# Weight-block sums formed on VectorE, their stores issued from GpSimd, token sums spread between products

## The chip, the cores and the metric

The kernel runs on one NeuronCore of a Trainium2 chip. Five engines work in parallel, each through its own instruction stream in order: TensorE (PE, the products), VectorE (DVE), ScalarE (ACT), GpSimd (POOL) and SyncE (SP, which here only issues DMAs). They meet through semaphores. The metric is the device time of one execution in microseconds (us), the median of the runs.

## The reference

Banded attention with distance biases on 4 batches, 8 heads, 768 positions and 64 elements a head, and then a feed-forward part on the 3072 tokens of 512 elements:

```python
scores = scale * np.matmul(q, k.transpose(0, 1, 3, 2)) + bias      # bias: -slope * distance
scores = np.where(keep, scores, -1000000000.0)                     # keep: first 8 keys, last 96 keys
a = np.exp(scores - max); a = a / (sum(a) + 1e-09)
x = (a @ v)                    # as 3072 x 512
h = (x @ w1) * (x @ w2) @ w3   # 512 -> 1024 -> 1024
out = h @ w_out                # 1024 -> 512
```

## The kernel before, in words

**Arithmetic.** Products are made of 32-bit values that are split in a high and a low half; a product of two such values is three products on TensorE (high by high, high by low, low by high). `w3 @ w_out` is multiplied out first (steps F), so a token needs only `x @ w1`, `x @ w2`, their elementwise product, and a product with the folded matrix.

**Units.** The tokens go in six units of 512. Units 0 and 1 multiply plainly: step `U.f.m.half` is half of the six 512-column products of feature block f (0 to 7) with `w1` (m = 0) or `w2` (m = 1). Results lie in a pool of four PSUM buffers (`m`); ScalarE copies the first (`gate`, tile `ag`), VectorE multiplies the second into it (`product`, L289), ScalarE and VectorE make its halves (`gh`, `gl`, L299). `Z.t.*` are the second products of the unit's t-th 128 tokens (L311 to L313), `ot` their copy and store. Units 2 to 5 (class `Sevenths`) use seven products of sums in place of eight: for that they need four sums of weight blocks (s1 to s4) beside the blocks, and sums of token blocks.

**Attention** runs ahead between the products. For score step s (two to a pair d = s // 2): `S.s` are the score products into the PSUM tiles `sc` and `more`, `R.s.q` the maxima on VectorE (L704), `E.s.q` the exponentials on ScalarE (L711), `s.s`, `c.s`, `X.s` the normalising and transposing on VectorE (L716, L717, L729, L737), and `V.d` the products with the values (L751), which leave x in `sc`. For units 0 and 1 `h.d` (ScalarE, L766) and `l.d` (VectorE, L771) make the halves `xh` and `xl`; only then may `sc` be overwritten by the next `S`. For later units `tokens(d)` copies x to `more_raws` and makes the blocks' sums and halves.

**Weight blocks.** In unit 0 each `w1`/`w2` block f is loaded, put together from 64-bit words (`convert`, L177 to L181), and split in halves `w12h`, `w12l`. Each is written to a DRAM buffer `ws` (`blocks_out`, four stores of 256 KB a block, on SP's queue). For the four sums, `rejoin(f)` adds the two halves back by two DMAs that GpSimd issues: one copies the high half to `block_sums`, the second adds the low half to it (L201, L202; the second waits for the first). `combine(f)` makes the four sums on VectorE (L208), ScalarE and VectorE halve them into `block_parts` (L211, L214), and `sums_out(f)` stores six pieces to `ws` on SP's queue (L219). `block_sums` has two buffers (f even, odd), `block_parts` holds the halves of one f. From unit 2 on `bring` loads blocks from `ws` (L239).

**Order.** TensorE's order is the program's order. Up to the end of unit 0 the table `ORDER` is the order on every engine, but a scheduler puts steps of later units between its steps where it takes an engine to be free. After it (`planned`) TensorE and ScalarE keep the written order; VectorE, SP and GpSimd are ordered by the scheduler. An engine that waits holds up all that stands behind the waiting instruction.

Of the kernel before, what the change touches and what calls it, by code (L numbers as in the profile page):

```python
# [20 lines left out]
P = 128  # L21
# [9 lines left out]
R = 32  # L31
# [53 lines left out]
class FeedForward:  # L85
# [485 lines left out]
def banded(ctx, tc, ff, ns, nt, n1, nf, oki, qk, vx, sc, pr):  # L571
# [203 lines left out]
    def tokens(d):  # L775

        u = d // 2
        raw = ff.tokens[:, d % 2]
        nc.scalar.activation(raw.rearrange("p (n t) -> p n t", t=T), sc[:, :, :T], AF.Copy)
        if d % 2 == 0:  # L780
            if u % 2 == 0:
                homes[u] = [ff.wf[1][:, k * 2048:(k + 1) * 2048] for k in range(4)]
            else:
                homes[u] = [xp.tile([P, 2048], F32R, tag=tag, name=f"{tag}{k}_{u}") for k in range(2) for tag in ("xh", "xl")]
        bh, bl, th, tl = homes[u]
        both = ff.tokens.rearrange("p d n -> p (d n)")
# [10 lines left out]
        halves(bh[:, 1024:1536], bl[:, 1024:1536], b22)  # L797
        halves(th[:, :512], tl[:, :512], b11)
        v.tensor_tensor(out=b12, in0=b22, in1=b12, op=ALU.subtract)
        v.tensor_tensor(out=b22, in0=b22, in1=b11, op=ALU.subtract)  # L800
        halves(th[:, 1024:], tl[:, 1024:], both[:, 1024:])
        v.tensor_tensor(out=b21, in0=b21, in1=b22, op=ALU.subtract)
        halves(th[:, 512:1024], tl[:, 512:1024], b21)
# [37 lines left out]

    def planned():

        def of(u, name):
            return lambda *x: getattr(units[u], name)(*x)

        last = NC // 2 - 1
        for f in range(NFC):
            for m in range(2):
                for half in range(2):  # L850
                    todo = [(of(1, "first"), f, m, half)]
                    if half:
                        todo += [(of(1, "gate"), f)] if m == 0 else [(of(1, x), f) for x in ("product", "high", "low")]
                    if m == 0 and half == 0:
                        todo.append((ff.blocks_out, f))
                    at = f * 4 + m * 2 + half
                    k = at // 5 + 1
                    if at % 5 == 0 and k < NFC:
                        todo.append((ff.combine, k))
                    if at % 5 == 1 and k < NFC:  # L860
                        todo += [(ff.sums_high, k), (ff.sums_low, k), (ff.sums_out, k)]
                        if k + 2 < NFC:
                            todo.append((ff.rejoin, k + 2))
                    if (f, m, half) in ((4, 0, 0), (7, 1, 1)):
                        todo += [(ff.bring, int(f == 7), g) for g in range(3)]
                    yield [("U", 1, f, m, half)] + todo
        for u in range(1, last + 1):
# [12 lines left out]
            for t in range(2 * T // P):  # L880
                for f in range(NFC):
                    todo = [(of(u, "third"), t, f)]
                    if f == NFC - 1:
# [4 lines left out]
                    if t == 0 and f in (1, 2) and tail:
                        yield tail.pop(0)
                    if t == 3 and f < 5 and u < last:  # L890
                        p = (1, 5, 6, 2, 7)[f]
                        yield [("P", u + 1, 0, p), (of(u + 1, "step"), p, 0)]

    with tc.manual_schedule(engines={mybir.EngineType.PE}):
        with tc.manual_schedule(engines={mybir.EngineType.DVE, mybir.EngineType.SP, mybir.EngineType.Activation, mybir.EngineType.Pool}):
            ordered()
        with tc.manual_schedule(engines={mybir.EngineType.Activation}):
# [22 lines left out]
            for d in range(STEPS // 2, n // 2):  # L920
                u = d // 2 - 1
                load(d)
                ahead = [s for s in (2 * d + 2, 2 * d + 3) if s < n]
                for s in ahead:
                    keys(s)
                rounds(d)
                go(place["Z", u, 2, 4] if d % 2 else place["U", u, 4, 0, 0] if u == 1 else place["P", u, 4, 1])
                values(d)
                tokens(d)
                if ahead:  # L930
                    go(place["Z", u, 3, 0] if d % 2 else place["Z", u, 0, 0] if u == 1 else place["P", u, 7, 4])
                for s in ahead:
                    scores(s)
# [44 lines left out]
```

## Time and profile before

| what | value |
|---|---|
| runs | 578.44 and 575.54 us, median 576.99 us |
| profiled execution | 577.99 us, its span 576.2 us, mean granted clock 0.967 |
| TensorE busy | 522.2 us, 91% of the span |
| VectorE busy | 344.4 us, 60% |
| ScalarE busy | 231.0 us, 40% |
| GpSimd busy | 16.5 us, 3% |
| DMA | 137.74 MB, mean 239 GB/s |

The profiled execution is 1.79 us longer than its span. TensorE's busy time includes stretches at half clock, so it is not all work at full speed. Times of instructions are given from the start of the span. In the trace the first product of unit 1 starts at 162.6 us and the first of unit 2 at 262.1 us; the other four units take what is left, 78.5 us each on the average.

### The profile page before, as it was taken

To read this page: it belongs to the slowest core of one execution; us is meant where nothing else is said; L and a number is where in the kernel's file an instruction comes from. 1 tells how busy PE (TensorE), PEld (TensorE's weight loads), DVE (VectorE), ACT (ScalarE), POOL (GpSimd) and SP (SyncE) were. 2 spreads that over 40 slices of the span, in tenths; PEclk is the share of its full clock that TensorE was granted. 3 is DMA by queue.
4 is the path that set the end of the run, shared out by engine and by line. 5 is a ranking of instruction groups with operands and counts; after the bars stand their busy time and mean duration, and the time that the engine had idled before them with its cause. 6 is when DMAs were issued, how large, how long until landed. Compare 5 with 4: busy or idle time off the path is not lost. (4 is left out here: it accounts for less than half of the span.)

```text
span 576.2 us, 14742 instructions
## 1 busy us (share of the span) xinstructions
PE 522.2 (91%) x6148; PEld 434.2 (75%) x6148; DVE 344.4 (60%) x886; ACT 231.0 (40%) x692; POOL 16.5 (3%) x45
## 2 busy tenths in 40 slices
PE   8999999995996797788999898999998899999997
PEld 5345478874884675677998787989787898789985
DVE  7999889945436634667545566545666357435520
ACT  2666746522342412545333435234354323433311
POOL 2000000010000101000000000000000000000000
PEclk9999999997998898799899899999999899999999
DMA  8997879973297878756699536789466887159801
GB/s 325 378 383 247 301 221 300 362 222 105 88 289 232 241 228 275 246 161 222 226 332 339 232 96 227 270 294 341 180 214 223 289 305 246 39 163 326 315 20 59
DMA packets 47644, 137.74 MB, mean 239 GB/s; under 512 B 4434, under 2 KB 22866, under 8 KB 45522
## 3 DMA queue, kind: packets, MB, share of 16 engines
q1 hardware_dynamic: 45120, 128.07, 64.2%
q0 software_dynamic: 2304, 8.39, 5.5%
q8 instruction: 50, 0.82, 0.6%
q10 hardware_dynamic: 146, 0.26, 0.1%
q14 instruction: 24, 0.20, 0.1%
HBM read 105.25 MB, written 23.07 MB: 223 GB/s over the span
## 5 line engine op out<-in xcount | busy, mean ns | idle before, releaser
L711 ACT ACTIVATE pr<-pr,mx 128x136 f32<-128x136 f32 (+2 forms) x192 | 74.5, 390 | 61.8 <-DVE mx L704 61.0
L311 PE MATMUL o<-wh,gh 128*128 128x512 f32 x184 | 73.7, 401 | 0.0
L312 PE MATMUL o<-wl,gh 128*128 128x512 f32 x184 | 72.2, 393 | 1.4 <-issue 1.4
L313 PE MATMUL o<-wh,gl 128*128 128x512 f32 x184 | 72.0, 391 | 0.0
L279 PE MATMUL m<-xh,w12h 128*128 128x512 f32 x128 | 52.0, 406 | 9.2 <-DVE ag L289 7.5
L388 ACT ACTIVATE ag<-x 128x256 f32<-128x256 f32 x64 | 24.3, 380 | 84.3 <-PE x L373 84.2
L373 PE MATMUL x<-w12l,w12h 128*128 128x256 f32 x384 | 54.8, 289 | 0.2
L373 PE MATMUL x<-xh,w12h 128*128 128x256 f32 x256 | 54.2, 289 | 0.5 <-ACT ag L388 0.2
L373 PEld LDWEIGHTS x<-w12l,w12h 128*128 128x128 f32 x384 | 50.7, 196 | 1.8 <-ACT ag L388 0.6
L299 DVE TENSOR_TENSOR gl<-ag,gh 128x512 fp32r<-128x512 f32 x48 | 33.0, 689 | 31.7 <-ACT gh L294 31.7
L280 PE MATMUL m<-xl,w12h 128*128 128x512 f32 x128 | 50.8, 397 | 0.0
L281 PE MATMUL m<-xh,w12l 128*128 128x512 f32 x128 | 50.8, 397 | 0.0
L294 ACT ACTIVATE gh<-ag 128x512 fp32r<-128x512 f32 x48 | 29.9, 624 | 49.3 <-DVE ag L289 39.6
L373 PE MATMUL y<-w12l,w12h 128*128 128x256 f32 x288 | 42.6, 294 | 6.0 <-ACT ot L325 5.4
L751 PE MATMUL sc<-pt,vr 32*64 32x160 f32 (+4 forms) x2112 | 35.8, 275 | 10.9 <-DVE pt L737 5.8
L751 PEld LDWEIGHTS sc<-pt,vr 32*64 32x64 f32 x2112 | 32.9, 136 | 16.7 <-issue 8.7
L373 PEld LDWEIGHTS x<-xh,w12h 128*128 128x128 f32 x256 | 43.6, 195 | 2.0 <-ACT ag L388 1.3
L373 PEld LDWEIGHTS y<-w12l,w12h 128*128 128x128 f32 x288 | 39.4, 202 | 7.0 <-ACT ot L325 5.8
L373 PE MATMUL y<-xh,w12h 128*128 128x256 f32 x192 | 40.7, 286 | 2.7 <-ACT ot L325 2.7
L313 PEld LDWEIGHTS o<-wh,gl 128*128 128x128 f32 x184 | 34.8, 189 | 9.1 <-issue 1.6
L311 PEld LDWEIGHTS o<-wh,gh 128*128 128x128 f32 x184 | 34.9, 190 | 7.5 <-issue 1.3
L312 PEld LDWEIGHTS o<-wl,gh 128*128 128x128 f32 x184 | 35.1, 191 | 6.0
(130 smaller groups left out, 888.8 us busy)
## 6 DMA issues: line engine op xcount, KB each, us to landing
w12h<-ws SPq DMA_DIRECT2D x64, 512.0 KB, 5.3
w12h<-ws SPq DMA_DIRECT2D x32, 768.0 KB, 6.4
qr<-qk SPq DMA_DIRECT2D x20, 720.0 KB, 8.8
vr<-vx SPq DMA_DIRECT2D x8, 768.0 KB, 4.4
out_dram<-ot SPq DMA_DIRECT2D x23, 256.0 KB, 2.0
raws<-w SPq DMA_DIRECT2D x5, 1024.0 KB, 6.4
ws<-w12h SPq DMA_DIRECT2D x16, 256.0 KB, 6.1
ws<-w12l SPq DMA_DIRECT2D x16, 256.0 KB, 6.9
```

The source lines that it names most:

```text
L279: self.nc.tensor.matmul(ps, lhsT=mh, rhs=xh[:, i], start=i == 0, stop=False)
L280: self.nc.tensor.matmul(ps, lhsT=mh, rhs=xl[:, i], start=False, stop=False)
L281: self.nc.tensor.matmul(ps, lhsT=ml, rhs=xh[:, i], start=False, stop=i == NCC - 1)
L294: self.nc.scalar.activation(self.gh[:, f], self.g[f], AF.Copy)
L299: self.nc.vector.tensor_tensor(out=self.gl[:, f], in0=self.g[f], in1=self.gh[:, f].bitcast(F32), op=ALU.subtract)
L311: self.nc.tensor.matmul(ps, lhsT=self.gh[:, f, ts], rhs=ff.wh[:, f], start=f == 0, stop=False)
L312: self.nc.tensor.matmul(ps, lhsT=self.gh[:, f, ts], rhs=ff.wl[f], start=False, stop=False)
L313: self.nc.tensor.matmul(ps, lhsT=self.gl[:, f, ts], rhs=ff.wh[:, f], start=False, stop=f == NFC - 1)
L373: self.nc.tensor.matmul(out, lhsT=w[:, i], rhs=x[:, i], start=p in (1, 5) and i == 0 and j == 0, stop=i == 1 and j == 2, skip_group_check= ...
L388: s.activation(e[(1, 6, 5).index(p)], y if p == 5 else x, AF.Copy)
L711: nc.scalar.activation(x, x, AF.Exp, bias=mx[:, q, u:u + 1], scale=-1.0, accum_out=sm[:, q, u:u + 1])
L751: nc.tensor.matmul(sc[cols, hp, n0 * R:n1 * R], lhsT=v[rows, i, cols], rhs=turned, start=i == i0, stop=i == NV - 1, skip_group_check=True)
```

## The change

`rejoin` with its two DMAs goes. `combine` begins with one VectorE instruction of 128x1024 that adds the two halves itself, for each of the eight blocks. `block_parts` now has two buffers for the high halves, and the low halves are written over `block_sums`. The stores of `blocks_out` and `sums_out`, 32 and 48 DMAs, are issued by GpSimd in place of SP. The table has `ps.0`, `sh.0`, `sl.0`, `so.0` (combine, halves, store of block 0) earlier, among R.6 to Z.1.2, and block 1 likewise among R.7 to Z.3.0; blocks 2 to 7 are planned into unit 1, each five half steps earlier than before, and the scheduler puts 2 and 3 into unit 0's end, 4 ahead of VectorE's product of block 1 and 5, 6 and 7 between its products of blocks 3 and 5. `V.d` with its `tokens` stands later for even d: in unit 1 four half steps later (before U.5.0.0), in later units seven products later. The second `tokens` of a unit is cut in three parts (`near`, `far`, `rest`) that are put at Z.2.5, Z.3.0 and Z.3.2.

```diff
-    def rejoin(self, f):
+    def combine(self, f):
         if f == 0:
             self.sums = self.xp.tile([P, 2, 4, 2 * P], F32, tag="xh", name="block_sums")
             self.parts = self.xp.tile([P, 2, 4, 2 * P], F32R, tag="xl", name="block_parts")
+        v = self.nc.vector
         hi, lo = (w[:, f].rearrange("p n i m -> p (n i m)").bitcast(F32) for w in self.w)
-        raw = self.sums[:, f % 2].rearrange("p k m -> p (k m)")
-        self.nc.gpsimd.dma_start(out=raw, in_=hi)
-        self.nc.gpsimd.dma_start(out=raw, in_=lo, accum_op=ALU.add)
-
-    def combine(self, f):
-
+        v.tensor_tensor(out=self.sums[:, f % 2].rearrange("p k m -> p (k m)"), in0=hi, in1=lo, op=ALU.add)
...
     def sums_high(self, f):
-        self.nc.scalar.activation(self.parts[:, 0], self.sums[:, f % 2], AF.Copy)
+        self.nc.scalar.activation(self.parts[:, f % 2], self.sums[:, f % 2], AF.Copy)
     def sums_low(self, f):
-        self.nc.vector.tensor_tensor(out=self.parts[:, 1], in0=self.sums[:, f % 2], in1=self.parts[:, 0].bitcast(F32), op=ALU.subtract)
+        x = self.sums[:, f % 2]
+        self.nc.vector.tensor_tensor(out=x.bitcast(F32R), in0=x, in1=self.parts[:, f % 2].bitcast(F32), op=ALU.subtract)
     def sums_out(self, f):
         for k0, k1, at in ((0, 1, slice(7, 8)), (1, 3, slice(4, 7, 2)), (3, 4, slice(2, 3))):
-            for h in range(2):
-                self.nc.sync.dma_start(out=self.ws[f, :, at, h], in_=self.parts[:, h, k0:k1].bitcast(F32))
+            for h, x in enumerate((self.parts[:, f % 2].bitcast(F32), self.sums[:, f % 2])):
+                self.nc.gpsimd.dma_start(out=self.ws[f, :, at, h], in_=x[:, k0:k1])
     def blocks_out(self, f):
...
-            self.nc.sync.dma_start(out=self.ws[f, :, 0:2, h], in_=x[:, 0])
-            self.nc.sync.dma_start(out=self.ws[f, :, 3:6:2, h], in_=x[:, 1])
+            self.nc.gpsimd.dma_start(out=self.ws[f, :, 0:2, h], in_=x[:, 0])
+            self.nc.gpsimd.dma_start(out=self.ws[f, :, 3:6:2, h], in_=x[:, 1])
...
+        later.extend((near, far, rest))
...
-                    k = at // 5 + 1
+                    k = at // 5 + 2
...
-                        if k + 2 < NFC:
-                            todo.append((ff.rejoin, k + 2))
...
+                    if u < last and (t, f) in ((2, 5), (3, 0), (3, 2)):
+                        todo.append((token_stage,))
...
-                go(place["Z", u, 2, 4] if d % 2 else place["U", u, 4, 0, 0] if u == 1 else place["P", u, 4, 1])
+                go(place["Z", u, 2, 4] if d % 2 else place["U", u, 5, 0, 0] if u == 1 else place["P", u, 5, 1])
```

VectorE before, at the start of unit 0's second products, up to the low half `xl` of the attention result of pair 2 (`l.2`); a row in brackets names the semaphores that the instruction waits for (DMASW: a DMA that GpSimd issued):

```order
L299 TENSOR_TENSOR gl_1029<-ag_6_1236,gh_1011 128x512 [waits Activation_49]
L289 TENSOR_TENSOR ag_7_1268<-m_7_1_1261,ag_7_1268 128x512 [waits PE_49,Activation_49]
L299 TENSOR_TENSOR gl_1029<-ag_7_1268,gh_1011 128x512 [waits Activation_49]
L208 TENSOR_TENSOR block_sums<-block_sums 128x256 [waits DMASW3_49]
L208 TENSOR_TENSOR block_sums<-block_sums 128x256 [waits DVE_49] x3
L771 TENSOR_TENSOR xl_1389<-sc,xh_1388 128x4x256 [waits Activation_49]
L704 ISA pr,mx_1472<-more_0_1400,bias_94 128x40 [waits PE_49]
```

The same place in the changed kernel:

```order
L286 TENSOR_TENSOR ag_6_1236<-m_6_1_1229,ag_6_1236 128x512 [waits PE_49,Activation_49]
L296 TENSOR_TENSOR gl_1029<-ag_6_1236,gh_1011 128x512 [waits Activation_49]
L286 TENSOR_TENSOR ag_7_1268<-m_7_1_1261,ag_7_1268 128x512 [waits PE_49,Activation_49]
L296 TENSOR_TENSOR gl_1029<-ag_7_1268,gh_1011 128x512 [waits Activation_49]
L768 TENSOR_TENSOR xl_1383<-sc,xh_1382 128x4x256 [waits Activation_49]
L701 ISA pr,mx_1466<-more_0_1394,bias_94 128x40 [waits PE_49]
```

The four sums of block 1, which waited for a DMA ahead of `xl`, are gone from here; `xl` follows the last `gl` directly.

VectorE before, from X.7 (the transposing of the last score step of pair 3) to the `xl` of pair 3, with which unit 1 can begin:

```order
L716 TENSOR_SCALAR sm_1534<-sm_1534 128x8 [waits Activation_49]
L717 RECIPROCAL sm_1534<-sm_1534 128x8 [waits DVE_49]
L729 TENSOR_TENSOR pr<-pr,sm_1534 128x8x136 [waits DVE_49]
L737 STREAM_TRANSPOSE pt_1517<-pr 128x8x5x32 [waits DVE_49]
L208 TENSOR_TENSOR block_sums<-block_sums 128x256 [waits DMASW1_49]
L208 TENSOR_TENSOR block_sums<-block_sums 128x256 [waits DVE_49] x3
L771 TENSOR_TENSOR xl_1389<-sc,xh_1388 128x4x256 [waits Activation_49]
L214 TENSOR_TENSOR block_parts<-block_sums,block_parts 128x1024 [waits Activation_49]
```

The same place in the changed kernel, from s.7 on:

```order
L713 TENSOR_SCALAR sm_1543<-sm_1543 128x8 [waits Activation_49]
L201 TENSOR_TENSOR block_sums<-w12h,w12l 128x1024 [waits DMASW5_49,DMASW3_49,DMASW1_49]
L714 RECIPROCAL sm_1543<-sm_1543 128x8 [waits DVE_49]
L204 TENSOR_TENSOR block_sums<-block_sums 128x256 [waits DVE_49]
L726 TENSOR_TENSOR pr<-pr,sm_1543 128x8x136 [waits DVE_49]
L204 TENSOR_TENSOR block_sums<-block_sums 128x256 [waits DVE_49]
L734 STREAM_TRANSPOSE pt_1519<-pr 128x8x5x32 [waits DVE_49]
L211 TENSOR_TENSOR block_sums<-block_sums,block_parts 128x1024 [waits Activation_49]
L204 TENSOR_TENSOR block_sums<-block_sums 128x256 [waits DVE_49] x2
L201 TENSOR_TENSOR block_sums<-w12h,w12l 128x1024 [waits DMASW7_49,DMASW3_49,DMASW1_49]
L204 TENSOR_TENSOR block_sums<-block_sums 128x256 [waits DVE_49] x3
L768 TENSOR_TENSOR xl_1383<-sc,xh_1382 128x4x256 [waits Activation_49]
```

Three times a 128x1024 sum of halves (L201) and its four sums (L204) now stand here, for blocks 1 (above the first row), 2 and 3. Those of blocks 2 and 3 wait for three DMAs each: the stores of the low halves of blocks 0 and 1, which lie in the buffers that they write. The first of them stands ahead of X.7, the second ahead of `xl`.

GpSimd before, its DMAs for the first three blocks (the rows above are of the program's start):

```order
L201 DMA block_sums<-w12h 128x1024 [waits DVE_49,Activation_49]
L202 DMA block_sums<-w12l 128x1024 [waits DMASW0_49]
L201 DMA block_sums<-w12h 128x1024
L202 DMA block_sums<-w12l 128x1024 [waits DMASW2_49]
L201 DMA block_sums<-w12h 128x1024 [waits DMASW1_49,DVE_49]
L202 DMA block_sums<-w12l 128x1024 [waits DMASW4_49]
```

In the changed kernel, the last of the 32 block stores and the first stores of sums:

```order
L222 DMA ws<-w12h 128x2x256 [waits DMASW5_49]
L221 DMA ws<-w12l 128x2x256 [waits DMASW6_49,DVE_49]
L222 DMA ws<-w12l 128x2x256 [waits DMASW7_49]
L216 DMA ws<-block_parts 128x256 [waits DMASW0_49,Activation_49]
L216 DMA ws<-block_sums 128x256 [waits DMASW1_49,DVE_49]
L216 DMA ws<-block_parts 128x2x256 [waits DMASW2_49]
L216 DMA ws<-block_sums 128x2x256 [waits DMASW3_49]
L216 DMA ws<-block_parts 128x256 [waits DMASW4_49]
L216 DMA ws<-block_sums 128x256 [waits DMASW5_49]
L216 DMA ws<-block_parts 128x256 [waits DMASW6_49,Activation_49]
```

The sums' stores stand behind all block stores; each waits for the eighth DMA before it, and high and low halves alternate.

## Rows read from the trace of the kernel before

**Rows 1.** The page: busy us, share of the span and instructions of each engine.

```profile
PE 522.2 (91%) x6148; PEld 434.2 (75%) x6148; DVE 344.4 (60%) x886; ACT 231.0 (40%) x692; POOL 16.5 (3%) x45
```

**Rows 2.** TensorE's timeline: start, us, work, in brackets the idle before and releaser.

```profile
135.74 0.60 PE L695 MATMUL sc<-qr 64*32 64x104 f32 x16 [7.01 <-DVE xl L771]
...
186.46 0.50 PE L279 MATMUL m<-xh,w12h 128*128 128x512 f32 x1 [1.73 <-ACT ag L286]
...
197.25 3.56 PE L751 MATMUL sc<-pt,vr 32*64 32x160 f32 x128 [4.07 <-DVE pt L737]
...
234.51 0.93 PE L695 MATMUL more<-qr 64*32 64x136 f32 x23 [5.64 <-DVE ag L289]
...
254.51 2.12 PE L751 MATMUL sc<-pt,vr 32*64 32x160 f32 x128 [1.47 <-DVE pt L737]
```

**Rows 3.** Who waited for whom: us in total, times, longest.

```profile
PE m L279 <- DVE ag L289: 7.5, 3, 3.8
...
DVE block_sums L208 <- DMA block_sums<-w12l: 39.4, 7, 13.0
...
ACT pr L711 <- DVE mx L704: 61.0, 21, 9.4
```

**Rows 4.** Mean granted TensorE clock (PEclk) in a window at the stall of 197 us.

```profile
197.00:199.00 2.00, 1.75 (x56) 1.75 (x64) 1.90 (x3) 0.06 (x1) 0.83 (x2) 0.51 0.90 294
```

**Rows 5.** VectorE's timeline, the places where it waited for block sums or halves.

```profile
132.74 1.80 DVE L208 TENSOR_TENSOR block_sums<-block_sums 128x256 f32<-128x256 f32 x4 [7.88 <-DMA block_sums<-w12l]
...
134.47 1.22 DVE L771 TENSOR_TENSOR xl<-sc,xh 128x1024 fp32r<-128x1024 f32 x1
...
176.66 1.80 DVE L208 TENSOR_TENSOR block_sums<-block_sums 128x256 f32<-128x256 f32 x4 [13.00 <-DMA block_sums<-w12l]
...
232.63 1.23 DVE L214 TENSOR_TENSOR block_parts<-block_sums,block_parts 128x1024 fp32r<-128x1024 f32 x1 [2.61 <-ACT block_parts L211]
```

**Rows 6.** ScalarE's timeline, the high half of the attention result.

```profile
125.46 1.03 ACT L766 ACTIVATE xh<-sc 128x1024 fp32r<-128x1024 f32 x1 [1.33 <-PE sc L751]
```

**Rows 7.** Unit 1's first products: length, busy us (x) PE, PEld, DVE, ACT, POOL, PEclk, ...

```profile
162.60:234.00 71.40, 52.99 (x388) 42.03 (x386) 32.45 (x72) 21.23 (x51) 8.04 (x11) 0.91 0.81 247
```

**Rows 8.** VectorE's timeline around the normalising steps s.6 and s.7.

```profile
140.73 0.17 DVE L716 TENSOR_SCALAR sm<-sm 128x8 f32<-128x8 f32 x1 [1.13 <-ACT pr L711]
...
144.05 0.30 DVE L704 CUSTOM_DVE_ANT_0 pr<-sc,biasw 128x136 f32<-128x136 f32 x1
...
145.81 0.08 DVE L704 DVE_READ_ACCUMULATOR2_ANT mx<- 128x1 f32 x1
...
150.22 0.17 DVE L716 TENSOR_SCALAR sm<-sm 128x8 f32<-128x8 f32 x1 [4.33 <-ACT pr L711]
...
151.98 1.51 DVE L737 STREAM_TRANSPOSE pt<-pr 128x1280 f32<-128x1280 f32 x1
```

**Rows 9.** TensorE's timeline in unit 0's second products.

```profile
138.54 0.71 PE L311 MATMUL o<-wh,gh 128*128 128x512 f32 x1
...
155.29 1.00 PE L751 MATMUL sc<-pt,vr 32*64 32x128 f32 x45
...
161.00 1.47 PE L695 MATMUL sc<-qr 64*32 64x136 f32 x85
```

**Rows 10.** GpSimd's timeline, DMA issues.

```profile
121.19 0.89 POOL L202 DMA_DIRECT2D block_sums<-w12l  x1 [5.48 <-DMA block_sums<-w12h]
...
121.77 0.85 POOL L201 DMA_DIRECT2D block_sums<-w12h  x1
```

**Rows 11.** DMA issues: count, KB each, median us to landing.

```profile
out_dram<-ot SPq DMA_DIRECT2D x23, 256.0 KB, 2.0
...
ws<-w12l SPq DMA_DIRECT2D x16, 256.0 KB, 6.9
...
ws<-block_parts SPq DMA_DIRECT2D x32, 128.0 KB, 3.7
```

**Rows 12.** VectorE's groups by line, to 165 us: busy us, mean ns of one.

```profile
L177 DVE TENSOR_SCALAR t3s<-raws 128x1024 int32<-128x1024 int32 x5 | 3.4, 689 | 2.0 <-DMA raws<-w 2.0
```

More of the change, by code (lines that the diff above doesn't have):

```diff
@@ L68 @@
 E.5.0 U.5.1.0 gl.4 a.5 R.5.3 E.5.1 wl.7 U.5.1.1 E.5.2 E.5.3 U.6.0.0 g.5 gh.5 s.5 U.6.0.1 c.5 X.5 U.6.1.0 a.6 U.6.1.1 gl.5 U.7.0.0 g.6 gh.6 U.7.0.1
-gl.6 U.7.1.0 a.7 U.7.1.1 pr.0 pr.1 V.2 g.7 gh.7 gl.7 Z.0.0 h.2 d.v3 l.2 Z.0.1 S.6 S.7 Z.0.2 R.6.0 d.q8 R.6.1 E.6.0 R.6.2 E.6.1 R.6.3 Z.0.3 E.6.2 E.6.3 Z.1.0
-ot.0 s.6 c.6 Z.1.1 X.6 Z.1.2 Z.1.3 d.q9 R.7.0 R.7.1 E.7.0 R.7.2 Z.2.0 ot.1 R.7.3 E.7.1 Z.2.1 E.7.2 E.7.3 Z.2.2 s.7 c.7 Z.2.3 X.7 ps.0 Z.3.0 ot.2 Z.3.1
-V.3 Z.3.2 h.3 sh.0 l.3 sl.0 so.0 pr.2 Z.3.3 ot.3
+gl.6 U.7.1.0 a.7 U.7.1.1 V.2 g.7 gh.7 gl.7 Z.0.0 h.2 d.v3 l.2 Z.0.1 S.6 S.7 Z.0.2 R.6.0 d.q8 R.6.1 E.6.0 R.6.2 E.6.1 R.6.3 ps.0 Z.0.3 E.6.2 E.6.3 sh.0 Z.1.0
+ot.0 s.6 c.6 Z.1.1 X.6 sl.0 so.0 Z.1.2 Z.1.3 d.q9 R.7.0 R.7.1 E.7.0 R.7.2 Z.2.0 ot.1 R.7.3 E.7.1 ps.1 Z.2.1 E.7.2 E.7.3 sh.1 Z.2.2 s.7 c.7 Z.2.3 X.7 sl.1 so.1 Z.3.0 ot.2 Z.3.1
+V.3 Z.3.2 h.3 l.3 Z.3.3 ot.3
 """
@@ L198, in rejoin @@
             self.parts = self.xp.tile([P, 2, 4, 2 * P], F32R, tag="xl", name="block_parts")
+        v = self.nc.vector
         hi, lo = (w[:, f].rearrange("p n i m -> p (n i m)").bitcast(F32) for w in self.w)
-        raw = self.sums[:, f % 2].rearrange("p k m -> p (k m)")
-        self.nc.gpsimd.dma_start(out=raw, in_=hi)
-        self.nc.gpsimd.dma_start(out=raw, in_=lo, accum_op=ALU.add)
-    def combine(self, f):
+        v.tensor_tensor(out=self.sums[:, f % 2].rearrange("p k m -> p (k m)"), in0=hi, in1=lo, op=ALU.add)
         a21, a22, a11, a12 = s3, s1, s2, s4 = [self.sums[:, f % 2, k] for k in range(4)]
         for out, x, y, op in ((s1, a21, a22, ALU.add), (s3, a11, a21, ALU.subtract), (s2, s1, a11, ALU.subtract), (s4, a12, s2, ALU.subtract)):
-            self.nc.vector.tensor_tensor(out=out, in0=x, in1=y, op=op)
+            v.tensor_tensor(out=out, in0=x, in1=y, op=op)
     def sums_high(self, f):
-        self.nc.scalar.activation(self.parts[:, 0], self.sums[:, f % 2], AF.Copy)
+        self.nc.scalar.activation(self.parts[:, f % 2], self.sums[:, f % 2], AF.Copy)
     def sums_low(self, f):
-        self.nc.vector.tensor_tensor(out=self.parts[:, 1], in0=self.sums[:, f % 2], in1=self.parts[:, 0].bitcast(F32), op=ALU.subtract)
+        x = self.sums[:, f % 2]
+        self.nc.vector.tensor_tensor(out=x.bitcast(F32R), in0=x, in1=self.parts[:, f % 2].bitcast(F32), op=ALU.subtract)
     def sums_out(self, f):
         for k0, k1, at in ((0, 1, slice(7, 8)), (1, 3, slice(4, 7, 2)), (3, 4, slice(2, 3))):
-            for h in range(2):
-                self.nc.sync.dma_start(out=self.ws[f, :, at, h], in_=self.parts[:, h, k0:k1].bitcast(F32))
+            for h, x in enumerate((self.parts[:, f % 2].bitcast(F32), self.sums[:, f % 2])):
+                self.nc.gpsimd.dma_start(out=self.ws[f, :, at, h], in_=x[:, k0:k1])
     def blocks_out(self, f):
@@ L796, in tokens, with near, far, rest @@
         v.tensor_tensor(out=b11, in0=b12, in1=b11, op=ALU.subtract)
[L797 to L803, printed above, removed]
+        def near():
+            halves(bh[:, 1024:1536], bl[:, 1024:1536], b22)
+            halves(th[:, :512], tl[:, :512], b11)
+            v.tensor_tensor(out=b12, in0=b22, in1=b12, op=ALU.subtract)
+            v.tensor_tensor(out=b22, in0=b22, in1=b11, op=ALU.subtract)
+        def far():
+            halves(th[:, 1024:], tl[:, 1024:], both[:, 1024:])
+            v.tensor_tensor(out=b21, in0=b21, in1=b22, op=ALU.subtract)
+        def rest():
+            halves(th[:, 512:1024], tl[:, 512:1024], b21)
+        later.extend((near, far, rest))
         at = dict(b11=(0, 0), b21=(0, 1), b22=(0, 2), t1=(1, 0), t4=(1, 1), t3=(1, 2), t2=(1, 3))
@@ L818, in sizes @@
         warm(0)
-    units, homes = {}, {}
-    do = dict(pr=ff.rejoin, ps=ff.combine, sh=ff.sums_high, sl=ff.sums_low, so=ff.sums_out, A=lambda *x: ff.convert(0, *x), B=lambda *x: ff.convert(1, *x), C=lambda *x: ff.convert(2, *x), wh=ff.high, wl=ff.low, F=ff.fold, pe=ff.fold_out, ph=ff.fold_high, pl=ff.fold_low, S=scores, R=maxima, E=exponentials, s=sums, c=lambda s: scale(s, nc.scalar if s < FIRST else nc.vector), X=turn, V=values, h=high, l=low, bias=distances, bD=masks, biasA=biases, nt=sizes)
+    units, homes, later = {}, {}, []
+    do = dict(ps=ff.combine, sh=ff.sums_high, sl=ff.sums_low, so=ff.sums_out, A=lambda *x: ff.convert(0, *x), B=lambda *x: ff.convert(1, *x), C=lambda *x: ff.convert(2, *x), wh=ff.high, wl=ff.low, F=ff.fold, pe=ff.fold_out, ph=ff.fold_high, pl=ff.fold_low, S=scores, R=maxima, E=exponentials, s=sums, c=lambda s: scale(s, nc.scalar if s < FIRST else nc.vector), X=turn, V=values, h=high, l=low, bias=distances, bD=masks, biasA=biases, nt=sizes)
     do.update((name, lambda *x, method=method: getattr(units[0], method)(*x)) for name, method in (("U", "first"), ("a", "gate"), ("g", "product"), ("gh", "high"), ("gl", "low"), ("Z", "second"), ("ot", "store")))
@@ L842, in planned, with token_stage @@
     def planned():
+        def token_stage():
+            later.pop(0)()
         def of(u, name):
```

## The prediction

> **What bounds the kernel now.** The profiled execution is the base: 577.99 us, 1.0 above the median of the runs shown. The page's shares come first: TensorE is busy for 522.2 us of the 576.2 us span, VectorE for 344.4, GpSimd for 16.5 [rows 1]. The bound is TensorE's work with its gaps, so I read TensorE's timeline next and noted each gap with its releaser, then asked in the list of waits and in VectorE's timeline why the releaser was late.
>
> At stake are these gaps: 7.01 us before S.6, put down to `xl`; 7.5 in three waits for VectorE's product `ag` (the longest 3.8); 1.73 for ScalarE's `ag`; 4.07 before V in unit 1; 5.64 before a score step, again for `ag` [rows 2, 3]. The sum is 25.9. VectorE is not short of time there: it waits for the second of GpSimd's two rejoining DMAs, 39.4 us in seven waits, 13.0 in the worst [rows 3, 5]. What TensorE needs is queued behind that wait. The first gap shows it best: VectorE idles 7.88 us, makes the four sums (1.80), and `xl` comes next at 134.47 [rows 5]. `xh` was there at 126.5 [rows 6], so `xl` could have been done by 127.7, before TensorE fell idle at 128.7. The whole 7.0 is the DMA's.
>
> A gap costs twice. At 197 us, right after a gap of 4.07, the granted clock is 0.51, the lower level of 1.2 GHz [rows 4], and the 128 products of V take 3.56 us; the same number takes 2.12 after a gap of 1.47 [rows 2]. So a long gap costs 1.44 more. I count five such (7.01; the 3.8; the rest of the 7.5; 4.07; 5.64): 7.2. **At stake: 33.1 us.**
>
> **The change part by part.** The two rejoining DMAs go, and with them VectorE's wait for them. VectorE gains eight 128x1024 sums. The nearest row, a 128x1024 instruction of two inputs, takes 1.23 [rows 5], so 1.2 each, 9.8 in all; with its four sums a `combine` is now 1.2 + 1.8 = 3.0. That alone costs nothing in unit 1: VectorE is busy for 32.5 of 71.4 us there [rows 7], and the cover is its idle time. SP sheds 80 issues, and nothing waited for it. The stores of whole blocks are read back only in unit 2 and stay off the path. V later in unit 1 takes away the 4.07, since `pt` is then long there.
>
> New costs come from position. `block_sums` now holds the low halves until they are stored, so the sum of block f+2 waits until GpSimd has issued block f's stores and they have landed. No row shows such a store from GpSimd. For the landing I take 3.7, the row of the same 128 KB from SP, with ends 2.0 and 6.9 [rows 11]. For the issue I take 0.75, between the 0.58 that separates two of GpSimd's issues and the 0.89 that one lasts [rows 10].
>
> *Gap at V.3* (in before's times; what matters is VectorE against TensorE, and both move up together). Block 0's `combine` falls on an idle of 1.13 before s.6 [rows 8], so it delays by 1.9; its low half adds 1.2: R.7 is 3.1 later, starting at 147.1 and over at 149.0 instead of 145.9 [rows 8]. Block 1's `combine` goes on to 152.0. Block 0's low half was ready at 147.1; four more issues of 0.75 and the landing of 3.7 give 153.8. Only then can the sum of block 2 run, which stands ahead of X.7: 1.2, then 0.2 + 0.45 + 1.3 + 0.45 and X.7's 1.5 come to 158.9. TensorE does unbroken work from 138.54 and reached V.3 at 155.29 [rows 9]. Gap **3.6**; with a landing of 6.9 it is 6.8. With none of the store's wait VectorE is still busy until 152.0 and the gap is 2.0, the low end.
>
> *Gap before unit 1.* After X.7 come block 1's low half 1.2, four issues 3.0, landing 3.7, the sum of block 3 1.2, three of the four sums 1.3, and `xl` 1.2: X.7 + 11.6. TensorE needs 5.7 from V.3 to the part of S.8 that overwrites `sc` (155.29 to 161.00) [rows 9]. Gap **5.9**, from 4.2 to 9.1 with the landing.
>
> *Unit 1.* Between the products of blocks 3 and 5 VectorE now has three `combine` (9.0), three low halves (3.7) and two half-size steps of block 4 (1.2 together): 13.9. TensorE can run two blocks ahead on four `m` buffers. Its work there is 52.99 busy less three slow spells of 1.44, 48.7 for eight blocks, so 12.2 for two [rows 7]. Gap 1.7, say **2.0**; it is 0 if the scheduler's order gives way elsewhere, and 5.7 with a landing of 3.7 on top. The score step behind the last product: **0.7**, about half of a 1.23 step, 0 to 1.2.
>
> *Clock.* Two new long gaps at 1.44: **2.9**; one gives 1.4, three 4.3.
>
> *Token sums.* The same instructions in three parts, now behind exponentials in VectorE's and ScalarE's way. ScalarE waits 61.0 us for maxima [rows 3], so a part put ahead of a maximum can delay the copy `ot`. Four unit borders by one 1.23 step are 4.9 at worst. Below nothing: the 1.47 before V at 254.5 [rows 2] may go. I take **1.0**, near nothing, since no work is added.
>
> The sum of new costs is 3.6 + 5.9 + 2.0 + 0.7 + 2.9 + 1.0 = 16.1; the gain 33.1 - 16.1 = 17.0, and 577.99 - 17.0 = **561.0 us**. All low ends: 2.0 + 4.2 + 0 + 0 + 1.4 - 1.5 = 6.1, which gives 551.0. All high ends: 6.8 + 9.1 + 5.7 + 1.2 + 4.3 + 4.9 = 32.0, which gives 576.9.
>
> The landing is where a page has its own price. The Trainium skill, page "DMA: Bandwidth & Descriptors", section "Anatomy of one DMA — SWDGE (gpsimd) path", fits a GpSimd-issued transfer as 2.0 us and its bytes over 436e3 per us, an estimate of 2.3 for 128 KB against the row's 3.7; by it the two gaps would be 1.4 each shorter, and the sum 558.2. The row is a median under this kernel's traffic, so it is the one I used.
>
> **The rivals.**
>
> *One DMA wait for another (0.25).* GpSimd's stores land as slowly as the slowest stores do here. For it: SP's own stores of low halves took 6.9 beside the same weight loads [rows 11], and these are issued beside the loads that unit 2 needs. Against it: these are half as large. V.3 6.8 and S.8 9.1 bring the sum to 22.5, so 567.4; with unit 1 at its 5.7 as well, 571.
>
> *GpSimd's queue becomes the bound (0.11), the slower side.* Place: the stores of sums, 48 where GpSimd issued 16 DMAs before, each in turn, and two a `combine` waits for. Price: at an issue of p, each 0.1 over 0.75 costs 0.4 at V.3 and 0.4 before unit 1. From p = 1.33 the 36 stores of blocks 2 to 7 exceed TensorE's 48.7 in unit 1, and that adds 36 p - 48.7. The gain is used up at p = 1.6 (6.8 + 8.9 of 17.0), and at p = 1.9 the costs are 9.2 + 19.7, so 561.0 + 28.9 = 590. For it: the issues in rows 10 are of large plain blocks, and a store into the gapped layout of `ws` may take longer to write. Against it: 0.58 to 0.89 is all that any row shows, and twice that is needed.
>
> *VectorE held up by GpSimd (0.06).* The block stores are now issued beside unit 0's conversions, of which eight are one-input instructions of 0.69 [rows 12]. If GpSimd's issue of 0.89 blocks one each time, unit 0, where VectorE feeds TensorE without slack, loses up to 8 x 0.89 = 7.1: 568. No row has the two side by side. The Trainium skill, page "SBUF — State Buffer", section "Who interferes with whom", states this lock: GpSimd and a VectorE copy or tensor_scalar in its two-port mode exclude each other for a whole instruction, and it advises against issuing DMAs from GpSimd beside them. It speaks against this change, and the traces of before cannot show it.
>
> *Stores land in 2.0 us (0.08).* Gaps of 2.0 and 4.2 bring 557.7, and with unit 1 clean 555.
>
> That the waits are only moved and nothing is gained would need both new gaps at their high ends and unit 1 at 5.7, which is the first rival with the token costs on top (577); its chance is in the 0.25.
>
> **How the numbers follow.** The forecast, 556 to 566, has 0.50. The range reaches over the fast rival and the two slow-store cases, from 551 to 577, the ends of the sum; outside lie GpSimd's queue as the bound and what I have not thought of. Two per cent (what can be told from no change) lies at 565.4 and 588.5. Faster: the forecast below 565.4 (0.48) and the fast landing (0.08), 0.56. Same: slow landing, blocked conversions and the rest of the forecast, 0.33. Slower: 0.11.
>
> **What would show it.** Right: no wait of VectorE for a DMA ahead of l.2 and TensorE unbroken up to V.3, a gap of 2 to 7 there whose chain runs X.7, the sum of block 2, a store of `block_sums`; another of 4 to 9 before S.8 behind `xl`; nothing before S.6. The 4.07 before V in unit 1 gone, and granted clock 0.5 only after those two gaps. Wrong in size: GpSimd's store issues over 1.3 apart, or landings off 3.7. Wrong in kind: VectorE's one-input conversions longer than 0.69 in unit 0, or gaps in units 2 to 5 that end on `ot` and were not there before.

## The result, and the profile of the changed kernel

557.69 us (557.60 to 557.79) against 576.99: a ratio of 0.967, with a 95% interval of 0.956 to 0.977. The forecast was 561.0 with 551 to 577, faster. The profiled execution took 557.79 us, 20.2 less than that of before; the forecast for it was 17.0.

Three stretches of the program hold all of that gain. The windows below run from the first product of S.6 to the first product of unit 1, from there to the score step behind unit 1's first products, from there to unit 2's first product, and to the end. Columns: length, busy us (and instructions) of PE, PEld, DVE, ACT, POOL, then the granted clock. Before:

```profile
128.30:162.59 34.29, 27.28 (x486) 22.55 (x485) 17.87 (x67) 11.28 (x41) 1.02 (x2) 0.90 0.38 119
162.59:228.45 65.86, 52.58 (x387) 41.91 (x384) 29.54 (x67) 20.19 (x50) 7.16 (x10) 0.92 0.81 249
228.45:262.14 33.69, 26.58 (x524) 21.96 (x524) 22.37 (x69) 14.72 (x44) 0.88 (x1) 0.90 0.66 202
262.14:576.20 314.06, 291.85 (x3446) 267.94 (x3445) 163.41 (x453) 116.06 (x360) 0.00 (x0) 0.98 0.66 227
```

The changed kernel:

```profile
128.90:166.68 37.78, 27.48 (x486) 22.39 (x485) 25.18 (x79) 13.15 (x47) 7.33 (x12) 0.89 0.46 153
166.68:216.41 49.73, 48.03 (x392) 39.28 (x385) 34.86 (x71) 19.77 (x45) 18.59 (x31) 0.98 0.63 220
216.41:241.79 25.38, 24.79 (x525) 20.43 (x524) 17.19 (x59) 13.36 (x46) 3.12 (x6) 1.00 0.45 157
241.79:555.90 314.11, 291.43 (x3446) 267.92 (x3444) 164.06 (x453) 116.52 (x356) 0.00 (x0) 0.98 0.65 226
```

Unit 0's end became 3.5 us longer, unit 1 16.1 and 8.3 shorter, units 2 to 5 are the same to 0.05. Over the first three rows TensorE's idle time (length less busy) falls from 27.4 to 12.6, and its busy time for the same products from 106.4 to 100.3.

TensorE's timeline of the changed kernel, its gaps in those stretches (start, us, work, in brackets the idle before and its releaser), which answer to [rows 2]:

```profile
150.12 2.12 PE L748 MATMUL sc<-pt,vr 32*64 32x160 f32 x128 [2.35 <-DVE pt L734]
...
163.77 2.98 PE L692 MATMUL sc<-qr 64*32 64x136 f32 x96 [7.95 <-DVE xl L768]
...
213.46 0.50 PE L276 MATMUL m<-xh,w12h 128*128 128x512 f32 x1 [1.70 <-DVE ag L286]
...
217.42 0.58 PE L692 MATMUL more<-qr 64*32 64x136 f32 x23 [0.59 <-DVE ag L286]
```

Of the gaps of [rows 2] only the one before the score step behind unit 1's first products is left, 0.59 where 5.64 stood; the 1.70 stands before the products of block 7 with `w2`, the last of unit 1's first products. Two new ones stand where they were forecast, before V.3 and before S.8. The second ends on `xl`, and VectorE's timeline shows what `xl` had waited for:

```profile
145.43 1.23 DVE L201 TENSOR_TENSOR block_sums<-w12h,w12l 128x1024 f32<-128x1024 f32 x1 [1.59 <-DMA ws<-block_sums]
...
148.56 1.50 DVE L734 STREAM_TRANSPOSE pt<-pr 128x1280 f32<-128x1280 f32 x1
149.99 1.18 DVE L211 TENSOR_TENSOR block_sums<-block_sums,block_parts 128x1024 fp32r<-128x1024 f32 x1
...
159.98 1.23 DVE L201 TENSOR_TENSOR block_sums<-w12h,w12l 128x1024 f32<-128x1024 f32 x1 [8.01 <-DMA ws<-block_sums]
161.24 1.34 DVE L204 TENSOR_TENSOR block_sums<-block_sums 128x256 f32<-128x256 f32 x3
162.50 1.22 DVE L768 TENSOR_TENSOR xl<-sc,xh 128x1024 fp32r<-128x1024 f32 x1
```

The sum of block 3 wants the buffer in which block 1's low half lies, and that half's stores went out late, since VectorE made the half only at 149.99, behind X.7. GpSimd's timeline, the first and the last of block 1's stores of low halves:

```profile
151.58 0.54 POOL L216 DMA_DIRECT2D ws<-block_sums  x1 [5.78 <-DVE block_sums L204]
...
154.14 0.55 POOL L216 DMA_DIRECT2D ws<-block_sums  x1
```

From 154.14 to VectorE's start at 159.98 are 5.84 us, while the median landing of low halves is 3.7 (the issues of the changed kernel, count, KB each, median us to landing):

```profile
ws<-block_parts POOLq DMA_DIRECT2D x16, 128.0 KB, 3.2
ws<-block_sums POOLq DMA_DIRECT2D x16, 128.0 KB, 3.7
```

SP's timeline shows what ran beside these stores: as soon as V.3 is done, SP loads the next values, 768 KB, which took 5.5 us.

```profile
152.27 0.34 SPq L662 DMA_DIRECT2D vr<-vx  x1
```

### The profile page after: what moved, and what is told of

Read it like the earlier page. It is cut to its first block, busy times and chain, and to the rows that moved or that the text cites. A ratio compares the mean times of both kernels' runs of the same rounds, so it can differ in the third digit from the quotient of the medians.

```text
span 555.9 us, 14759 instructions
## 1 busy us (share of the span) xinstructions
PE 515.7 (93%) x6148; PEld 430.4 (77%) x6148; DVE 353.8 (64%) x894; ACT 231.8 (42%) x692; POOL 57.1 (10%) x109
## 5 line engine op out<-in xcount | busy, mean ns | idle before, releaser
L276 PE MATMUL m<-xh,w12h 128*128 128x512 f32 x128 | 50.8, 397 | 1.7 <-DVE ag L286 1.7
L748 PEld LDWEIGHTS sc<-pt,vr 32*64 32x64 f32 x2112 | 31.1, 130 | 11.5 <-issue 7.4
L748 PE MATMUL sc<-pt,vr 32*64 32x160 f32 (+4 forms) x2112 | 33.3, 266 | 6.3 <-issue 3.9
```

What stands on the lines that cost most here:

```text
L276: self.nc.tensor.matmul(ps, lhsT=mh, rhs=xh[:, i], start=i == 0, stop=False)
L748: nc.tensor.matmul(sc[cols, hp, n0 * R:n1 * R], lhsT=v[rows, i, cols], rhs=turned, start=i == i0, stop=i == NV - 1, skip_group_check=True)
```

## The experiments

What the profile of the changed kernel could not tell is which of its parts brings the gain. My theory behind the sum was that the rejoining DMA caused what was lost, and that the two new waits are made by where the low halves lie and when their stores land. Rivals: the new places or the later V bring the gain; GpSimd's queue costs by itself; the waits only move. Ratios are to the kernel before, run beside each kernel, with 95% intervals. Runs of one kernel here spread by up to 2%, so only differences of over about 1.5% are read. Line numbers differ by a few between kernels.

**dve_only: one part of the change alone.** The steps `pr`, which issued the two DMAs, go from the table and the plan with it (not shown).

```diff
 the kernel before, with
-        self.nc.gpsimd.dma_start(out=raw, in_=hi)
-        self.nc.gpsimd.dma_start(out=raw, in_=lo, accum_op=ALU.add)
+        self.nc.vector.tensor_tensor(out=self.sums[:, f % 2].rearrange("p k m -> p (k m)"), in0=hi, in1=lo, op=ALU.add)
```

Expected: 

> The kernel before with one part of the change: VectorE adds the halves of each block in place of the two rejoining DMAs; places in table and plan, buffers, stores on SP, V and token sums as before. Theory: the rejoining DMA was the cause of nearly all that was lost, so most of the 20 us comes with this part alone: 556 to 563 us, with the gap of 4 before V in unit 1 still there. Rival: the sum alone is worth little because one buffer of halves and the old places leave VectorE waiting for stores instead, and the rest of the change brings the gain: 567 to 574 us.

Measured: 537.44 us, 0.935 (0.931 to 0.939), so better than the theory's own range, and 3% better than the whole change. The same windows of its trace, the first three:

```profile
127.95:153.63 25.68, 25.68 (x486) 21.34 (x485) 17.28 (x59) 10.64 (x38) 0.00 (x0) 1.00 0.40 138
153.63:201.49 47.86, 47.01 (x387) 38.66 (x384) 40.58 (x92) 22.91 (x55) 0.00 (x0) 1.00 0.78 261
201.49:226.01 24.52, 24.52 (x525) 20.39 (x524) 16.89 (x58) 12.78 (x41) 0.00 (x0) 1.00 0.59 183
```

TensorE is idle for 0.85 us in all of it, and the clock is whole. So this part takes away nearly everything that was at stake in these stretches, and it needs no other part. It also gives the price of the clock: the same products kept TensorE busy for 97.2 us here and for 106.4 before, so 9.2 us of slow clock. What is idle is this gap before V in unit 1:

```profile
177.46 2.11 PE L745 MATMUL sc<-pt,vr 32*64 32x160 f32 x128 [0.85 <-DVE pt L731]
```

V stands at its old place, and of the 4.07 of [rows 2] only 0.85 is left. The expected gap of 4 isn't there.

**no_vshift, no_split: two parts taken out of the changed kernel.** In no_split the three places in the plan go too (not shown).

```diff
-  place["U", u, 5, 0, 0] if u == 1 else place["P", u, 5, 1]
+  place["U", u, 4, 0, 0] if u == 1 else place["P", u, 4, 1]
```

Expected: 

> The changed kernel with V.d for even d back at its old places (before U.4.0.0, and P.4.1 in later units). Theory: V in unit 1 waits for pt again, 4.07 and 1.44 of slow clock: 561 to 564 us. Rival: VectorE no longer waits for DMAs, so pt is early enough and the shift was worth nothing: 556.5 to 559 us.

Measured: 554.44 us, 0.963 (0.954 to 0.971), below both ranges and nearer to the rival. The theory falls: with V at its old place this gap is

```profile
189.29 2.12 PE L748 MATMUL sc<-pt,vr 32*64 32x160 f32 x128 [0.60 <-DVE pt L734]
```

```diff
-        later.extend((near, far, rest))
+        near()
+        far()
+        rest()
```

Expected: 

> The changed kernel with the second token stage of a unit in one piece again, at its old place. Theory: the split moved nothing that TensorE waits for: 556.5 to 559 us. Rival: the long piece holds up maxima and ot, so the split had been worth 3 to 5 us: 560.5 to 563 us.

Measured: 556.63 us, 0.967 (0.963 to 0.972): nothing, as the theory had it.

**dve_vshift, dve_split: the same two parts put into dve_only.**

Expected: 

> dve_only with V.d of even d at the changed places. Theory: pt is there anyway once VectorE does not wait for DMAs, so nothing in unit 1, and in units 2 to 5 the later V costs up to 4: 537 to 542 us. Rival: the later V takes away small waits for pt: 533 to 536 us.

Measured: 540.19 us, 0.940 (0.935 to 0.946). The interval touches that of dve_only, so no gain is shown, and whether the later V costs some 3 us stays open: units 2 to 5 take 315.0 us in its trace and 312.2 in dve_only's, but each is one execution.

Expected: 

> dve_only with the second token stage cut in three parts at the changed places. Theory: nothing on the path moves, 536 to 539 us. Rival: the parts leave VectorE free for maxima and for ot's place: 532 to 535 us.

Measured: 538.28 us, 0.937 (0.933 to 0.942): nothing.

**late: the sums of blocks 2 and 3 behind `xl`.** The plan leaves these two blocks out (not shown).

```diff
-V.3 Z.3.2 h.3 l.3 Z.3.3 ot.3
+V.3 Z.3.2 h.3 l.3 ps.2 sh.2 Z.3.3 ot.3 sl.2 so.2 ps.3
```

Expected: 

> The changed kernel with the sums of weight blocks 2 and 3 moved behind the low half of pair 3 (l.3), by the table. Theory: the gaps of 2.35 us before V.3 and 7.95 before the score step S.8 are nothing but VectorE waiting there for stores of block_sums; both go, with some 2 us of slow clock behind the second, and unit 1 pays back at most 3: 545 to 549 us. Rival: VectorE has no room for them later, the same waits come back before the products of unit 1: 553 to 558 us.

Measured: 551.52 us, 0.959 (0.954 to 0.964), between the two. Both gaps of unit 0 are gone, the first window is 25.69 long with a whole clock, and unit 1 gives most of it back. Windows of `late`:

```profile
127.27:152.96 25.69, 25.69 (x485) 21.33 (x485) 21.15 (x60) 11.15 (x39) 7.33 (x12) 1.00 0.56 192
152.96:211.62 58.66, 51.60 (x387) 41.25 (x384) 39.65 (x92) 22.78 (x56) 20.21 (x34) 0.91 0.60 207
```

Unit 1's first products take 58.7 in place of 49.7. The wait is the same one, now of the sum of block 4 for block 2's stores, ahead of VectorE's product `ag` of block 0 (VectorE's timeline of `late`):

```profile
166.04 1.23 DVE L201 TENSOR_TENSOR block_sums<-w12h,w12l 128x1024 f32<-128x1024 f32 x1 [6.05 <-DMA ws<-block_sums]
167.18 0.68 DVE L286 TENSOR_TENSOR ag<-m,ag 128x512 f32<-128x512 f32 x1
```

TensorE's longest gap there ends on ScalarE's copy, which stands behind exponentials that had waited 4.38 us for VectorE's late maxima; that these are late by the same wait is read from the order, and no run tests it.

```profile
175.12 0.79 PE L276 MATMUL m<-xh,w12h 128*128 128x512 f32 x1 [4.16 <-ACT ag L283]
```

So a later place doesn't remove it. The next three kernels take away its two causes.

**old_buffers, sp_stores, sp_old_buffers: the buffer and the queue.** In the first, high and low halves go to `block_parts` again and `block_sums` is free once they are made; in the second, SP issues the 80 stores; in the third, both. Of each edit some lines are shown, the others are of the same kind.

```diff
 old_buffers
-        self.nc.vector.tensor_tensor(out=x.bitcast(F32R), in0=x, in1=self.parts[:, f % 2].bitcast(F32), op=ALU.subtract)
+        self.nc.vector.tensor_tensor(out=self.parts[:, 1], in0=self.sums[:, f % 2], in1=self.parts[:, 0].bitcast(F32), op=ALU.subtract)
 sp_stores (three lines like this)
-                self.nc.gpsimd.dma_start(out=self.ws[f, :, at, h], in_=x[:, k0:k1])
+                self.nc.sync.dma_start(out=self.ws[f, :, at, h], in_=x[:, k0:k1])
```

Expected: 

> The changed kernel with the old use of block_parts: high and low halves of one block lie there, and block_sums is free again as soon as its halves are made. Everything else as changed (places, GpSimd's queue, V, token stage). Theory: the two gaps in unit 0 are made by the low halves lying in block_sums until they are stored; the 7.95 goes and the 2.35 shrinks to about 1: 545 to 549 us. Rival: the early places alone fill VectorE ahead of X.7 and xl, and a store still waits somewhere: 554 to 558 us.

Expected: 

> The changed kernel with all 80 block stores issued by SP again, everything else as changed (places, low halves over block_sums, V, token stage). Theory: the same stores land sooner from SP (2.4 and 3.2 us in dve_only, 4.5 and 5.9 from GpSimd in dve_pool), so VectorE's waits shrink: the gap before V.3 to about 1, the 7.95 before S.8 to 4 or 5: 547 to 552 us. Rival: the wait is set by where the low halves lie, not by who issues the store: 555 to 558 us.

Expected: 

> The changed kernel with SP's stores and the old use of block_parts; what is left of the change beside VectorE's sums are the early places, V and the token stage. Theory: the queue and the buffer explain what the change lost against dve_only, so 537 to 542 us. Rival: the early places cost by themselves: 544 to 548 us.

Measured, with the changed kernel as the fourth corner; all three lie in the ranges of the theory:

| low halves | stores by GpSimd | stores by SP |
|---|---|---|
| over `block_sums` (changed) | 0.967 (0.956 to 0.977) | 0.952 (0.942 to 0.963), 551.22 us |
| in `block_parts` (old) | 0.951 (0.945 to 0.958), 546.22 us | 0.935 (0.925 to 0.944), 540.74 us |

From corner to corner the ratios differ by 1.4 to 1.8%. Only in the lower row do the intervals stand apart; in the other three steps they touch or overlap, and the traces carry the reading. The three stretches last 112.9 us in the changed kernel, 105.1 in sp_stores, 105.0 in old_buffers and 98.4 in sp_old_buffers. So each of the two costs 6.6 to 7.9 us there, and together they cost what the whole change lost against dve_only (98.1).

The corner without either (0.935) has the early places, the later V and the split token stage, and it is no better and no worse than dve_only: with SP's stores those parts are worth nothing that can be measured. With GpSimd's stores they are worth something: old_buffers (0.951) and dve_pool below (0.964, 0.958 to 0.970) differ in these parts alone, the intervals stand apart, and the three stretches take 105.0 and 114.2 us. Which of the parts does it was not tried. The gap before S.8 in TensorE's timeline of sp_stores:

```profile
158.37 2.97 PE L692 MATMUL sc<-qr 64*32 64x136 f32 x96 [5.48 <-DVE xl L768]
```

It is 5.48 where GpSimd's stores made it 7.95, and in sp_old_buffers and in old_buffers there is none there. SP's timeline of sp_stores has the last store of the low half and then the load of values:

```profile
151.52 0.44 SPq L216 DMA_DIRECT2D ws<-block_sums  x1
...
152.55 0.40 SPq L662 DMA_DIRECT2D vr<-vx  x1
```

SP issues in order, so here the load goes out behind the stores, and the last of them let VectorE go after 2.6 us (154.12); in the changed kernel the load went out between GpSimd's stores, and it was 5.84. That the load made the difference is argued from this order; no run moves the load alone. In old_buffers another wait of TensorE remains, of 4.6 us before the score step behind unit 1's first products; there ScalarE's copy of high halves waits for a store instead (its timeline):

```profile
203.38 1.06 ACT L207 ACTIVATE block_parts<-block_sums 128x1024 fp32r<-128x1024 f32 x1 [4.64 <-DMA ws<-block_parts]
```

**dve_pool, dve_pool_blocks: the queue alone.** dve_only with all 80 stores from GpSimd, and with the 32 of whole blocks alone.

```diff
 dve_pool (in dve_pool_blocks, the second pair only)
-                self.nc.sync.dma_start(out=self.ws[f, :, at, h], in_=self.parts[:, h, k0:k1].bitcast(F32))
+                self.nc.gpsimd.dma_start(out=self.ws[f, :, at, h], in_=self.parts[:, h, k0:k1].bitcast(F32))
-            self.nc.sync.dma_start(out=self.ws[f, :, 0:2, h], in_=x[:, 0])
+            self.nc.gpsimd.dma_start(out=self.ws[f, :, 0:2, h], in_=x[:, 0])
```

Expected: 

> The kernel before with VectorE's sums (dve_only), and all 80 block stores issued by GpSimd in place of SP. Theory: who issues them does not matter to the path, 536 to 540 us. Rival: GpSimd's issue of 0.55 to 0.73 us in turn, or its descriptor writing beside unit 0's one-input conversions, holds up VectorE or the halves: 542 us or more.

Measured: 552.07 us, 0.964 (0.958 to 0.970): the rival's time. Of its reasons the one beside the conversions falls with the next run; the halves are held up, and what the trace shows there is the later landing of the stores.

Expected: 

> dve_only with the 32 stores of whole blocks alone issued by GpSimd; the 48 stores of sums stay on SP. Theory: nothing waits for the whole blocks until unit 2, and the 15 us of dve_pool came from the stores of sums: 536 to 540 us. Rival: GpSimd's issues beside VectorE's conversions or ahead of the sums cost part of it: 543 to 550 us.

Measured: 539.32 us, 0.931 (0.920 to 0.942), the theory. So the stores of whole blocks cost nothing that can be measured, and the loss came with the stores of sums (those 48 alone were not given to GpSimd). With one buffer of halves, ScalarE's next copy waits until stores of the halves before it have landed. The waits and the issues in dve_only:

```profile
ACT block_parts L205 <- DMA ws<-block_parts: 4.1, 3, 2.2
```

```profile
ws<-block_parts SPq DMA_DIRECT2D x32, 128.0 KB, 2.4
...
ws<-block_parts SPq DMA_DIRECT2D x16, 256.0 KB, 3.2
```

and in dve_pool:

```profile
ACT block_parts L205 <- DMA ws<-block_parts: 21.7, 6, 5.5
```

```profile
ws<-block_parts POOLq DMA_DIRECT2D x32, 128.0 KB, 4.5
...
ws<-block_parts POOLq DMA_DIRECT2D x16, 256.0 KB, 5.9
```

The same 48 transfers land 2 to 3 us later from GpSimd, and 21.7 us of waiting in six places take the place of 4.1 in three. The whole blocks went the other way. Their low halves landed in dve_only and then in dve_pool as follows, and their high halves in 6.2 and 4.8:

```profile
ws<-w12l SPq DMA_DIRECT2D x16, 256.0 KB, 6.3
...
ws<-w12l POOLq DMA_DIRECT2D x16, 256.0 KB, 3.7
```

So GpSimd's stores are not slower everywhere: in the same pair of kernels they are the quicker ones for whole blocks and the slower ones for sums.

## Why the prediction was right, step by step

**The mechanism and the size.** The bound, the cause of the gaps and the two new waits before V.3 and S.8 were as predicted. Idle time of TensorE in the three stretches: 27.4 to go (25.9 predicted, without the 1.47 before V that went too), 12.6 new (3.6 + 5.9 + 2.0 + 0.7 = 12.2 predicted; 2.35 + 7.95 + 1.70 + 0.59 measured). Slow clock: 9.2 to go (7.2 predicted; five spells came as counted, but they cost some 1.8 each where 1.44 was taken), 3.1 left, as 100.3 - 97.2 (2.9 predicted). Token sums: 0.05 (1.0 predicted). The terms move the forecast of 17.0 by +1.5, -0.4, +2.0, -0.2 and +1.0, and the later start of S.6 (128.9 for 128.3) by -0.6: 20.3, the 20.2 measured.

**Where the fit is luck.** The 2.9 of slow clock was two short spells. No spell followed the gap of 2.35, and the one behind the 7.95 was longer than any before: 5.13 us of work at a granted clock of 0.50 (the rows stand in the last section). The 2.7 in unit 1 (2.0 and 0.7) was priced as VectorE's own work, but VectorE also waited there for stores, four times and 7.8 us of this sum of the changed kernel:

```profile
DVE block_sums L201 <- DMA ws<-block_sums: 17.4, 6, 8.0
```

With the same work of VectorE and SP's stores, unit 1's first products have no gap at all, and there is none before the score step behind them (sp_stores, the second window):

```profile
161.27:208.48 47.21, 47.21 (x393) 38.98 (x385) 36.30 (x73) 21.00 (x47) 0.00 (x0) 0.99 0.73 242
```

So the 1.70 and the 0.59 were the stores' too. And units 2 to 5 last between 306.7 and 316.3 us in the thirteen traces here, each one execution, so that they agree to 0.05 is chance.

**Terms mis-sized.** The gap before S.8 was 7.95 for 5.9, since the last store took 5.84 to let VectorE go where 3.7 was taken from the row of SP's stores [rows 11]; it stayed inside the end of 9.1, which took 6.9. The gap before V.3 was 2.35 for 3.6: block 0's last low store was issued at 141.99 and let VectorE go at 145.43, 3.4 later, and its four issues took 2.6 where 3.0 was taken. VectorE's steps from there to the end of X.7 took 4.6 for 5.1, and the first 16 products of V.3 (0.47) ran before TensorE had to wait. The issue of a store of sums is 0.54 to 0.73, so the estimate of 0.75 was just above it, and GpSimd, issuing for 18.6 of the 49.7 us, never was the bound of unit 1. Two slips in the sum of the rival *GpSimd's queue becomes the bound* change nothing: 48.7 / 36 is 1.35, not 1.33, and at p = 1.6 the 15.7 leaves 1.3 of the 17.0.

**A step that failed.** "V later in unit 1 takes away the 4.07" was wrong in its reason: dve_only and no_vshift have V at the old place, and the gap there is 0.85 and 0.60. The 4.07 came from VectorE's wait for the rejoining DMA like the others; X stood behind it on VectorE (timeline of before; from 189.82 to 197.19 VectorE works without a gap):

```profile
189.82 1.34 DVE L208 TENSOR_TENSOR block_sums<-block_sums 128x256 f32<-128x256 f32 x3 [2.69 <-DMA block_sums<-w12l]
...
195.69 1.50 DVE L737 STREAM_TRANSPOSE pt<-pr 128x1280 f32<-128x1280 f32 x1
```

The sum did not feel it, because the 4.07 went either way: for this term, that is luck.

**The rivals.** *VectorE held up by GpSimd* didn't happen: dve_pool_blocks issues the 32 block stores from GpSimd in unit 0 and measures like dve_only, and the one-input conversions last 690 ns (VectorE's group in dve_pool_blocks, to 165 us; 689 in [rows 12]), though only four of the eight ran beside an issue:

```profile
L177 DVE TENSOR_SCALAR t3s<-raws 128x1024 int32<-128x1024 int32 x5 | 3.5, 690 | 0.6 <-DMA raws<-w 0.6
```

The lock that the Trainium skill's page "SBUF — State Buffer", section "Who interferes with whom", describes is not seen in these durations. One issue may have been held up: the one at 85.89 in dve_pool_blocks, with a conversion of 0.64 inside it, took 1.03 us where its neighbours took 0.72 to 0.75, and at the same place it took 1.02 in the changed kernel and 1.03 in dve_pool; no run shows what made it longer. *One DMA wait for another* came near its price in one of its two places (7.95, against 9.1 at its high end; 2.35 against 6.8 in the other), which is not enough for 567. The Trainium skill's fit for a GpSimd-issued transfer (page "DMA: Bandwidth & Descriptors", section "Anatomy of one DMA — SWDGE (gpsimd) path"), 2.3 us for 128 KB as an estimate, is under every median measured here for 128 KB from GpSimd (3.1 to 4.5 in the six traces that have them); the row of before was the better price.

**What the prediction did not ask.** It summed the change as one thing. By parts, VectorE's sums alone give 0.935, and the queue and the buffer give back nearly half of that gain. Both prices stood in the sum (12.2 of new idle time and 2.9 of clock), so a version without any of the new gaps could have been priced at 561.0 - 12.2 - 2.9 = 545.9 before any run. dve_only, at 537.4, beats both kernels. What stays open: whether the load of values is all that made the store before S.8 take 5.84, and why GpSimd's stores of sums land later than SP's while those of whole blocks land sooner.

## What to carry to other kernels

Price the parts of a change apart: the part that removes a wait may be the whole gain, and the parts that come with it may bring back waits of the same kind. When a buffer is reused as the source of a store, its next writer inherits the store's issue queue and landing; a later place for that write only moved the wait here (late), so give the store a buffer of its own and the queue on which its landing was measured as the shorter one in that place. A gap on TensorE is worth more than its length while a spell at the lower clock follows it.

## What the runs showed of the hardware

The 48 stores of sums landed in a median of 2.4 us (128 KB) and 3.2 us (256 KB) when SP issued all block stores (dve_only), in 4.5 and 5.9 us when GpSimd did (dve_pool). The 32 stores of whole blocks landed in 6.2 and 6.3 us from SP (dve_only) and in 5.1 and 4.5 from GpSimd (dve_pool_blocks, where nothing else moved). After the gap of 2.35 us the 128 products of V ran in 2.12 us at a granted clock of 1.00, the 2.4 GHz level; after the 7.95 the granted clock was 0.50, the 1.2 GHz level, for the next 5.13 us of TensorE's work (windows of the changed kernel):

```profile
150.12:152.24 2.12, 2.12 (x129) 2.08 (x129) 1.81 (x3) 0.00 (x0) 0.66 (x2) 1.00 0.00 0
...
163.77:168.90 5.13, 5.13 (x101) 4.31 (x102) 2.70 (x25) 1.68 (x8) 0.00 (x0) 0.50 0.55 179
```

In before the five such stretches were of 3.0 to 3.5 us of work; the longest, behind the 5.64:

```profile
234.51:237.90 3.39, 3.39 (x119) 3.38 (x126) 1.80 (x5) 1.09 (x2) 0.00 (x0) 0.50 1.04 329
```

In before a gap of 4.07 was followed by the lower clock [rows 2, 4], and in dve_pool one of 2.05 as well: the 128 products of V behind it took 3.61 us at a granted clock of 0.53 (TensorE's timeline, then the window).

```profile
182.03 3.61 PE L745 MATMUL sc<-pt,vr 32*64 32x160 f32 x128 [2.05 <-DVE pt L731]
...
182.03:185.64 3.61, 3.61 (x129) 3.57 (x129) 0.73 (x1) 1.54 (x2) 0.36 (x1) 0.53 0.23 86
```

So the length of one gap does not tell whether the clock falls; in dve_pool a gap of 3.02 us had ended 8.75 us before V's products start, and the clock was 1.00 between the two gaps.
